# An attention block with a gated feed-forward network: row sums transposed with the mixed tile, a decoding step merged, and a new order

## The chip, the core and the metric

The kernel runs on one core of one Trainium2 chip. The metric is the device time of one execution in microseconds (us). A kernel's time is the median of its runs; the profile is one more execution, with its own time.

The core has engines that each take their instructions in order from a queue of their own and wait for each other by semaphores: TensorE (PE in the profile; PEld is its loading of weights), VectorE (DVE), ScalarE (ACT), GpSimd (POOL) and SyncE (SP), which here issues most of the DMAs.

## What is computed

For 8 batches of 8 heads, 576 positions and head size 64, the reference rotates q and k, takes the softmax of their scaled products, multiplies by v, and sends the result through a feed-forward network with a causal gate of five taps:

```python
    q_rot, k_rot = (rotate(q), rotate(k))
    scale = 1.0 / np.sqrt(D)
    scores = scale * np.matmul(q_rot, k_rot.transpose(0, 1, 3, 2))
    scores = scores - np.max(scores, axis=-1, keepdims=True)
    attn = np.exp(scores)
    attn = attn / (np.sum(attn, axis=-1, keepdims=True) + 1e-09)
    return np.matmul(attn, v).astype(np.float32)
...
    x = np.ascontiguousarray(attn_out.transpose(0, 2, 1, 3)).reshape(B, S, H * D)
...
    for k in range(K):
        gate_pre += conv_w[k][None, None, :] * xp[:, k:k + S, :]
    gate = 1.0 / (1.0 + np.exp(-gate_pre))
    val = x @ w_val
    return (gate * val @ w_out).astype(np.float32)
```

The weights w_val, conv_w and w_out come as float64. The kernel reads their bits as pairs of 32-bit integers and builds float32 from them on the chip: this is "the decoding".

## The kernel before

**Pairs and batches.** Two heads make a pair; there are 32 pairs, four to a batch. A pair's 576 queries of each head are cut into nine tiles of 128 rows: four for each head, and one *mixed* tile (`pm`) that holds the last 64 queries of both heads. For each tile PE computes the scores (`s_mm`, L304: products of high and low parts, half the rows of PE for each head, 128 x 288), DVE takes the negative row maximum (`s_max`, L310), ACT takes the exponential into a tile `p` and adds each row up into a column of `sums` (`s_exp`, L323).

**Transposes.** P has to be transposed for the product with v. PE does it against the identity (`ident`, L338) into a bank of PSUM named `ps_t`; ACT (L379) or DVE (L381) copies the bank to the tiles `pt0` and `pt1`. The keys of a tile go in four pieces of 128 (`t0` to `t7`, `tm`); the remaining 64 keys of each head in the transposes `th0`, `th1` (keys of four tiles) and `thm` (`hm`, for the mixed tile: one transpose of its last 128 keys, of which the lower 64 rows are used).

**Row sums.** When all nine columns of a pair's sums are there, DVE adds 1e-9 and takes the reciprocal (`r_inv`, L404 and L405), PE transposes the 128 x 128 tile `sums` into a bank of its own (`r_mm`, L409, `ps_r`), ACT copies 16 rows (`r_copy`, L415), SP writes nine rows to DRAM and reads them back, spread over the partitions, into `rb` (`r_write`, `r_read`: one write and three reads). The last pair does this in two groups.

**Product with v and network.** `pv_mm` (L393, `ps_a`) multiplies with v, DVE normalises with `rb` into `x` (L432), ACT and POOL split x into a high and a low part (`xh`, `xl`), ACT and DVE compute the gate (L454, L457, L462). When a batch's four pairs are done, the network's first product runs on PE in 96 matmuls (`f_mm`, L480, `ps_f<-xh,wval_hi` and the like), DVE multiplies with the gate (L488), ACT and POOL split y (L492, L495), and 96 matmuls more give the output (`ps_f<-y,wout_hi`), scaled by ACT (L502) or DVE (L504). All of `ps_t`, `ps_r`, `ps_a` and `ps_f` share four banks in turn.

**Rotation.** q and k arrive by DMA in `qin` and `kin`; POOL, and for a part DVE, multiply and add (L276, L280), ACT and POOL or DVE split the result (L283, L287).

**Decoding.** `decode` (L516 to L530) builds float32 from the bits in seven steps, then splits it into `w_hi` (ACT) and `w_lo`. Steps four and five compare the exponent with the smallest normal one (L520) and multiply by the answer (L521). Steps five, nine and ten run on DVE or POOL, by a flag for each block. w_val comes in four blocks of 512 columns, w_out in eight of 256.

**The order.** No engine's order is written out. Every step is a job with an engine, a duration as the planner sees it, what it reads and writes, and a due time. The planner plays the jobs through and writes down the order in which each engine takes them; the due times and the choices of engine come from the table `DUE` (L30) and, for pairs 0 to 4 and batch 0, from its entries with `@e`. Where the planner sees PE idle in the first part of the run, it writes transposes of the identity into the gap (`fill`, L331), called fillers below. So a change of `DUE` changes the order on every engine, and neither arithmetic nor data.

Of the kernel before, what the change touches and what calls it, by code (L numbers as in the profile page):

```python
# [10 lines left out]
F32 = mybir.dt.float32  # L11
# [4 lines left out]
ALU = mybir.AluOpType  # L16
# [3 lines left out]
S = 576  # L20
D = 64
# [180 lines left out]
def attn_gated_ffn(ctx: ExitStack, tc: tile.TileContext, q2, k2, v2, tab, w_val, conv_w, w_out, out, collect=None):  # L202
# [42 lines left out]
    state = {}  # L245
# [66 lines left out]
    def s_exp(p, i):  # L312
        st = state[p]
        if i < 8:
            c, h = i // 2, i % 2
            if f"p{c}" not in st:
                st[f"p{c}"] = pp.tile([128, 2, S], F32, name="p", tag="p")
            pd = st[f"p{c}"][:, h]
            col = c + 5 * h
        else:  # L320
            pd = st["pm"] = pp.tile([128, 2, S], F32, name="p", tag="p")[:, 0]
            col = 4
        A.activation(out=pd.rearrange("p (b x) -> p b x", b=2), in_=st[f"s{i}"], func=AF.Exp, bias=st[f"nm{i}"], scale=1.0,  # L323
                     accum_out=sums[p % 2][:, col:col + 1])
# [16 lines left out]
    def t_mm(p, key):  # L341


        st = state[p]
        if key == "m":
            transpose(p, key, [(st["pm"][:, j * 128:(j + 1) * 128], 128) for j in range(4)])
        elif key == "hm":
            transpose(p, key, [(st["pm"][:, 448:S], 128)])
        elif key[0] == "h":
            g = int(key[1])  # L350
            transpose(p, key, [(st[f"p{2 * g + n}"].rearrange("p h s -> p (h s)")[:, 512:640], 128) for n in range(2)])
        else:
            c, h = int(key) // 2, int(key) % 2
            transpose(p, key, [(st[f"p{c}"][:, h, h * D + j * 128:h * D + (j + 1) * 128], 128) for j in range(4)])

    def t_copy(p, key, eng):
        st = state[p]
        bank = st["b" + key]
        g = 1 if key in ("m", "hm", "h1", "4", "5", "6", "7") else 0
        n = G1 if g else G0  # L360
        if f"pt{g}" not in st:
            st[f"pt{g}"] = pt.tile([128, 9 * n], F32, name=f"pt{g}", tag=f"pt{g}")
        t = st[f"pt{g}"]
        last = t[:, 8 * n:9 * n]
        if key == "m":
            moves = [(bank.rearrange("p (j h x) -> p j h x", j=4, h=2),
                      t[:, 0:8 * n].rearrange("p (h j x) -> p j h x", h=2, j=4)[:, :, :, 256:320])]
        elif key == "hm":
            moves = [(bank[D:128, HEAD[h]], last[HEAD[h], 256:320]) for h in range(2)]
        elif key[0] == "h":  # L370
            moves = [(bank[:, 0:256], last[:, 0:256])]
        else:
            c, h = int(key) // 2, int(key) % 2
            off = (c - 2 * g) * 128
            moves = [(bank.rearrange("p (j x) -> p j x", j=4),
                      t[:, 0:8 * n].rearrange("p (s x) -> p s x", x=n)[:, h * 4:h * 4 + 4, off:off + 128])]
        for src, dst in moves:
            if eng is A:
                A.copy(out=dst, in_=src)  # L379
            else:  # L380
                V.tensor_copy(out=dst, in_=src)  # L381
# [19 lines left out]
    def r_inv(p, g):  # L401
        for a, b in COLS[g]:
            r = sums[p % 2][:, a:b]
            V.tensor_scalar(out=r, in0=r, scalar1=1e-9, scalar2=None, op0=ALU.add)  # L404
            V.reciprocal(out=r, in_=r)  # L405
# [6 lines left out]
    def r_copy(p, g):  # L412
        st = state[p]
        st[f"rr{g}"] = small.tile([16, 128], F32, name="rr", tag="rr", bufs=B["rr"])
        A.copy(out=st[f"rr{g}"], in_=st[f"br{g}"][0:16, 0:128])  # L415
# [94 lines left out]
    def decode(st, fa, eng, hi_out=None, lo_out=None, whole=None):  # L510

        view = st.rearrange("p (n t) -> p n t", t=2)
        hi, lo = view[:, :, 1], view[:, :, 0]
        fh, wa = hi.bitcast(F32), fa.bitcast(I32)
        steps = [
            lambda: V.tensor_scalar(out=wa, in0=hi, scalar1=0x07FFFFFF, scalar2=3, op0=ALU.bitwise_and,  # L516
                                    op1=ALU.logical_shift_left),
            lambda: V.scalar_tensor_tensor(out=wa, in0=hi, scalar=-0x40000000, in1=wa, op0=ALU.bitwise_and, op1=ALU.bitwise_or),
            lambda: V.tensor_scalar(out=hi, in0=hi, scalar1=0x7FF00000, scalar2=None, op0=ALU.bitwise_and),
            lambda: V.tensor_scalar(out=fh, in0=hi, scalar1=float(0x38100000), scalar2=None, op0=ALU.is_ge),  # L520
            lambda: eng.tensor_tensor(out=fa, in0=fa, in1=fh, op=ALU.mult),  # L521
            lambda: V.tensor_scalar(out=hi, in0=wa, scalar1=-0x00800000, scalar2=None, op0=ALU.bitwise_and),
            lambda: V.scalar_tensor_tensor(out=fh, in0=lo.bitcast(U32), scalar=2.0 ** -52, in1=fh, op0=ALU.mult, op1=ALU.mult),  # L523
        ]
        if whole is not None:
            return steps + [lambda: V.tensor_tensor(out=whole, in0=fa, in1=fh, op=ALU.add)]
        return steps + [
            lambda: A.copy(out=hi_out, in_=fa),
            lambda: eng.tensor_tensor(out=fa, in0=fa, in1=hi_out.bitcast(F32), op=ALU.subtract),
            lambda: eng.tensor_tensor(out=lo_out, in0=fa, in1=fh, op=ALU.add),  # L530
        ]
# [67 lines left out]
    for i in range(8):  # L599
        at("dtap", 5.3 + 0.4 * i, "G" if i == 4 else "V", 190 if i == 4 else 90, lambda i=i: taps[i](), w="cw oo/taps0 oo/taps1",  # L600
           port=i in (1, 6, 7))

    def weights(n):
        for i in range(4 if n == "val" else 8):
            x = 512 if n == "val" else 256
            tok = f"y{1 - i % 2}/w{i}" if n == "val" else f"wst/{i}"
            at(f"l{n}{i}", 0, "SP", 650, load_weight, n, i, w=tok, kb=x * 1.024)
            v, v2, g = x * 0.522 + 67, x * 1.045 + 67, x * 2.18 + 105
            eg = ("V", v2) if O.get(f"e{n}{i}") else ("G", g)
            for k, (e, ns) in enumerate((("V", v), ("V", v2), ("V", v), ("V", v), eg, ("V", v), ("V", v2),  # L610
                                         ("A", x * 0.83 + 94), eg, eg)):
                at(f"d{n}{i}", k * 0.5, e, ns, weight_step, n, i, k, w=tok + f" w{n}{i}" * (k in (7, 9)), port=e == "V")

    for p in range(NP):
# [32 lines left out]
        for c in range(5):  # L647
# [154 lines left out]
```

## Time and profile before

| | us |
|---|---|
| median of 3 runs | 789.59 (788.5 to 789.95) |
| the profiled execution | 784.94 |
| its span, first to last instruction | 783.2 |
| busy in it: PE / DVE / ACT / POOL | 750.3 / 606.9 / 488.6 / 415.9 |

A profile's row of a group gives line, engine, operation, what is written and read, shape and count, then the busy time of the group, the mean duration in ns, and the engine's idle time just ahead of it with what ended it. A row of the timeline begins with start and duration in us. A row of waits gives engine and tile, what was waited for, and then the total in us, the number of waits and the longest. PE's matmuls overlap: the next one starts while the one before still runs, so its cost is the step from start to start and not its duration.

### The profile page before, as it was taken

To read this page: it belongs to the slowest core of one execution; us is meant where nothing else is said; L and a number is where in the kernel's file an instruction comes from. 1 tells how busy PE (TensorE), PEld (TensorE's weight loads), DVE (VectorE), ACT (ScalarE), POOL (GpSimd) and SP (SyncE) were. 2 spreads that over 40 slices of the span, in tenths; PEclk is the share of its full clock that TensorE was granted. 3 is DMA by queue.
4 is the path that set the end of the run, shared out by engine and by line. 5 is a ranking of instruction groups with operands and counts; after the bars stand their busy time and mean duration, and the time that the engine had idled before them with its cause. 6 is when DMAs were issued, how large, how long until landed. Compare 5 with 4: busy or idle time off the path is not lost.

```text
span 783.2 us, 16858 instructions
## 1 busy us (share of the span) xinstructions
PE 750.3 (96%) x6284; PEld 616.0 (79%) x6284; DVE 606.9 (77%) x994; ACT 488.6 (62%) x1155; POOL 415.9 (53%) x300
## 2 busy tenths in 40 slices
PE   8889789899999999999999999999999999999998
PEld 8766666578778887887778787887878788878798
DVE  5898989999877887778687887778687876876640
ACT  2565647556566676766666766766666766766532
POOL 2556535455666664567555664467556664551121
PEclk9999989999999999999999999999999999999999
DMA  7654313432343333432443343323343334410111
GB/s 189 158 123 128 82 45 94 127 82 73 90 116 94 94 101 95 108 84 64 116 116 101 89 112 102 102 72 71 109 116 107 91 106 110 114 30 24 33 42 62
DMA packets 92884, 73.81 MB, mean 94 GB/s; under 512 B 60633, under 2 KB 71426, under 8 KB 92802
## 3 DMA queue, kind: packets, MB, share of 16 engines
q1 hardware_dynamic: 91250, 71.51, 34.4%
q10 hardware_dynamic: 1552, 1.21, 0.7%
q8 instruction: 50, 0.82, 0.4%
q14 instruction: 32, 0.26, 0.1%
HBM read 63.10 MB, written 9.59 MB: 93 GB/s over the span
## 4 chain that ended last, share of the span: by engine, by line
PE 67%; DVE 21%; DMA 4%; ACT 4%; issue 3%; SPq 1%; POOL 1%; POOLq 0%; ACTq 0%; DVEq 0%
PE ps_f L480 21%; PE ps_a L393 15%; PE ps_s L304 14%; PE ps_t L338 14%; DVE nm L310 5%; DVE g L457 5%; ACT p L323 2%; DMA kin<-in_k 2%; DVE sums L404 2%; DVE pt L381 1%; PE ps_t L331 1%; DMA qin<-in_q 1%; DVE y L488 1%; DVE k L287 1%; DVE wst L523 1%
## 5 line engine op out<-in xcount | busy, mean ns | idle before, releaser
L323 ACT ACTIVATE p<-ps_s,nm 128x576 f32<-128x576 f32 x288 | 211.9, 739 | 117.2 <-DVE nm L310 114.7
L310 DVE TENSOR_REDUCE nm<-ps_s 128x1 f32<-128x576 f32 x288 | 208.9, 750 | 53.7 <-PE ps_s L304 52.3
L338 PE MATMUL ps_t<-ident,p 128*128 128x128 f32 x1312 | 191.4, 279 | 15.7 <-ACT p L323 9.5
L338 PEld LDWEIGHTS ps_t<-ident,p 128*128 128x128 f32 x1312 | 146.2, 141 | 50.5 <-issue 20.4
L304 PE MATMUL ps_s<-k,q 64*128 64x288 f32 (+1 forms) x1728 | 172.5, 309 | 4.3 <-ACT p L323 3.1
L393 PE MATMUL ps_a<-pt,v 128*64 128x320 f32 (+1 forms) x1280 | 170.5, 411 | 0.0
L304 PEld LDWEIGHTS ps_s<-k,q 64*128 64x128 f32 (+1 forms) x1728 | 135.2, 185 | 33.7 <-issue 18.9
L276 POOL TENSOR_TENSOR qin<-qin,tab_q 128x640 f32<-128x640 f32 x62 | 102.3, 1660 | 95.6 <-DMA qin<-in_q 95.6
L379 ACT COPY pt<-ps_t 128x512 f32<-128x512 f32 (+2 forms) x261 | 118.8, 466 | 27.5 <-PE ps_t L338 24.8
L393 PEld LDWEIGHTS ps_a<-pt,v 128*64 128x64 f32 x1280 | 85.8, 136 | 60.9 <-issue 10.1
L457 DVE SCALAR_TENSOR_TENSOR g<-x,cw,g 128x576 f32<-128x576 f32 (+2 forms) x132 | 118.2, 899 | 1.7 <-ACT g L454 1.4
L480 PE MATMUL ps_f<-y,wout_hi 128*128 128x288 f32 (+2 forms) x512 | 111.1, 304 | 2.4 <-ACT pt L379 2.4
L381 DVE COPY pt<-ps_t 128x512 f32<-128x512 f32 (+1 forms) x155 | 97.0, 629 | 10.3 <-PE ps_t L338 10.2
L287 POOL TENSOR_TENSOR q<-qin,q 128x640 fp32r<-128x640 f32 (+1 forms) x32 | 52.7, 1648 | 69.3 <-ACT q L283 63.9
L480 PEld LDWEIGHTS ps_f<-y,wout_hi 128*128 128x128 f32 x512 | 82.5, 189 | 5.0 <-ACT pt L379 3.5
L444 POOL TENSOR_TENSOR xl<-x,xh 128x576 fp32r<-128x576 f32 (+2 forms) x33 | 45.6, 1383 | 73.1 <-ACT xh L440 59.9
L495 POOL TENSOR_TENSOR y<-y,y 128x288 fp32r<-128x288 f32 (+2 forms) x64 | 54.2, 848 | 54.2 <-ACT y L492 54.1
L480 PE MATMUL ps_f<-xh,wval_hi 128*128 128x288 f32 (+2 forms) x256 | 77.9, 304 | 0.4 <-DVE x L432 0.3
L480 PE MATMUL ps_f<-xl,wval_hi 128*128 128x288 f32 (+2 forms) x256 | 77.2, 302 | 0.0
L480 PE MATMUL ps_f<-y,wout_lo 128*128 128x288 f32 (+2 forms) x256 | 77.1, 301 | 0.0
L480 PE MATMUL ps_f<-xh,wval_lo 128*128 128x288 f32 (+2 forms) x256 | 76.0, 297 | 0.0
L280 POOL TENSOR_TENSOR kin<-kin 128x640 f32<-128x640 f32 (+1 forms) x32 | 49.9, 1558 | 34.9 <-DVE kin L276 34.0
(74 smaller groups left out, 886.1 us busy)
## 6 DMA issues: line engine op xcount, KB each, us to landing
kin<-in_k SPq DMA_DIRECT2D x62, 288.0 KB, 3.9
qin<-in_q SPq DMA_DIRECT2D x31, 512.0 KB, 4.1
out_t<-o SPq DMA_DIRECT2D x56, 144.0 KB, 2.6
rb<-rd SPq DMA_DIRECT2D x31, 144.0 KB, 3.6
v<-in_v SPq DMA_DIRECT2D x32, 128.0 KB, 2.2
v<-in_v SPq DMA_DIRECT2D x64, 64.0 KB, 2.3
rb<-rd SPq DMA_DIRECT2D x31, 128.0 KB, 3.1
qin<-in_q SPq DMA_DIRECT2D x64, 32.0 KB, 3.0
```

Of the source, the lines that this page charges most:

```text
L276: eng.tensor_tensor(out=t[:, i, a:b], in0=t[:, i, a:b], in1=tabs[n][:, i, a:b], op=ALU.mult)
L287: eng.tensor_tensor(out=t[:, 1], in0=ins[n][:, 0, a:b], in1=t[:, 0].bitcast(F32), op=ALU.subtract)
L304: T.matmul(out=tiles[h][:, half, 0:288], lhsT=st["q"][rows, x, c * 128:c * 128 + 128], rhs=st["k"][rows, y, k0:k0 + 288], start=(i == 0), ...
L310: V.tensor_reduce(out=st[f"nm{i}"], in_=st[f"s{i}"], axis=AX.XY, op=ALU.max, negate=True)
L323: A.activation(out=pd.rearrange("p (b x) -> p b x", b=2), in_=st[f"s{i}"], func=AF.Exp, bias=st[f"nm{i}"], scale=1.0, accum_out=sums[p % 2 ...
L338: T.transpose(out=bank[0:rows, j * 128:(j + 1) * 128], in_=src, identity=ident)
L379: A.copy(out=dst, in_=src)
L381: V.tensor_copy(out=dst, in_=src)
L393: T.matmul(out=acc[HEAD[h], 0:n], lhsT=st["v"][:, j, h, :], rhs=st[f"pt{g}"][:, at_:at_ + n], start=(j == 0), stop=(j == 4))
L457: V.scalar_tensor_tensor(out=g, in0=x_sb[:, a + k:b + k], scalar=w, in1=g, op0=ALU.mult, op1=ALU.add)
L480: T.matmul(out=acc[:, 0:n], lhsT=wt[w][:, kc, ds], rhs=mv, start=(kc == 0 and i == 0), stop=(kc == NCH - 1 and i == 2))
L495: G.tensor_tensor(out=ffn[b][1][:, dc, lo:hi], in0=ffn[b, "y", dc, lo], in1=ffn[b][0][:, dc, lo:hi].bitcast(F32), op=ALU.subtract)
```

## The change

**Row sums.** For every pair but the last the reciprocal now goes to nine columns behind the mixed tile's keys (the tile's second half is free), and the transpose `hm` takes the mixed tile's last 64 keys and these nine columns together: 73 columns, one bank. Its rows 0 to 63 go to `pt1` as before, its rows 64 to 72 are the transposed sums that ACT copies for the write. The separate transpose stays only in the last pair. The transpose `hm` now also waits for the reciprocal, and the reciprocal stands in the list of jobs ahead of the transposes.

**Decoding.** Comparison and product are one `scalar_tensor_tensor` on DVE (12 blocks of weights, and the taps).

**Plan.** Of the 431 numbers in `DUE`, 317 are others, and 75 are new. Among them are choices of engine: from pair 5 on the copy of `t1` goes from DVE to ACT (27 copies), of the output scalings DVE has 39 in place of 22 and ACT the fewer, one block of w_val and one of w_out go from POOL to DVE in the decoding and another of w_out the other way, and in pair 0 some halves of the rotation change between DVE and POOL. There are 398 fillers in place of 395.

```diff
-            transpose(p, key, [(st["pm"][:, 448:S], 128)])
+            n = D if p == NP - 1 else D + 9
+            transpose(p, key, [(st["pmt"].rearrange("p h s -> p (h s)")[:, 512:512 + n], n)])
...
-            moves = [(bank[D:128, HEAD[h]], last[HEAD[h], 256:320]) for h in range(2)]
+            moves = [(bank[0:D, HEAD[h]], last[HEAD[h], 256:320]) for h in range(2)]
...
-            V.reciprocal(out=r, in_=r)
+            V.reciprocal(out=r if p == NP - 1 else state[p]["pmt"][:, 1, a:b], in_=r)
...
-        A.copy(out=st[f"rr{g}"], in_=st[f"br{g}"][0:16, 0:128])
+        if p == NP - 1:
+            A.copy(out=st[f"rr{g}"], in_=st[f"br{g}"][0:16, 0:128])
+        else:
+            A.copy(out=st[f"rr{g}"][0:9], in_=st["bhm"][D:D + 9, 0:128])
...
-            lambda: V.tensor_scalar(out=fh, in0=hi, scalar1=float(0x38100000), scalar2=None, op0=ALU.is_ge),
-            lambda: eng.tensor_tensor(out=fa, in0=fa, in1=fh, op=ALU.mult),
+            lambda: V.scalar_tensor_tensor(out=fa, in0=hi, scalar=float(0x38100000), in1=fa, op0=ALU.is_ge, op1=ALU.mult),
...
+        last = p == NP - 1
+        if not last:
+            at("rinv", t, "V", 450, r_inv, p, None, r=toks(f"sums{par}#@", range(9)) + f" p/{p}.m", w=f"p/{p}.m#r sums{par}#r")
...
-                r = f"p/{p}.m"
+                r = f"p/{p}.m" + f" p/{p}.m#r" * (key == "hm" and p < NP - 1)
```

Three places of the order show what moves. On PE, in the middle of the run, at the end of a pair's transposes (`ps_r` is the transpose of the sums, the single `ps_t` behind it is `hm`, `ps_f` is the network), before:

```order
L304 MATMUL ps_s<-k_86,q_88 128x288 x12
L338 MATMUL ps_t<-ident,p 128x128 x4
L409 MATMUL ps_r<-ident,sums_102 128x128
L338 MATMUL ps_t<-ident,p 128x128
L480 MATMUL ps_f<-xh,wval_hi 128x288
L480 MATMUL ps_f<-xl,wval_hi 128x288
```

and now, at a like place (`73x128` is `hm` with the sums):

```order
L304 MATMUL ps_s<-k_86,q_88 128x288 x12
L339 MATMUL ps_t<-ident,p 128x128 x4
L339 MATMUL ps_t<-ident,p 73x128
L485 MATMUL ps_f<-y_5410,wout_hi 128x288
L485 MATMUL ps_f<-y_5411,wout_hi 128x288
```

The transpose of the sums is gone, and the one behind it stands where it stood.

On PE in the opening, the network's first matmul, before: it stands behind scores of the seventh pair (360 score matmuls ahead of it) and the product with v of the sixth (`ps_a`).

```order
L409 MATMUL ps_r<-ident,sums_102 128x128
L338 MATMUL ps_t<-ident,p 128x128 x4
L393 MATMUL ps_a<-pt_1833,v_92 64x256 x4
L304 MATMUL ps_s<-k_86,q_88 128x288 x12
L393 MATMUL ps_a<-pt_1833,v_92 64x256 x6
L338 MATMUL ps_t<-ident,p 128x128 x4
L393 MATMUL ps_a<-pt_1938,v_92 64x320 x10
L304 MATMUL ps_s<-k_86,q_88 128x288 x12
L480 MATMUL ps_f<-xh,wval_hi 128x288
```

Now it stands behind the fifth pair's last scores (270 score matmuls ahead of it); the row without `p` is a filler:

```order
L304 MATMUL ps_s<-k_86,q_88 128x288 x12
L332 MATMUL ps_t<-ident 128x128 x15
L339 MATMUL ps_t<-ident,p 128x128 x4
L304 MATMUL ps_s<-k_86,q_88 128x288 x6
L339 MATMUL ps_t<-ident,p 128x128 x6
L485 MATMUL ps_f<-xh,wval_hi 128x288
```

The network begins 90 score matmuls earlier in PE's queue.

On DVE, the last piece of w_val's low part (`wval_lo`), which the network's first matmul needs; `nm` is a row maximum, `g` a tap of the gate, `wst` a block under decoding. Before it is the 259th instruction, behind 58 maxima:

```order
L523 SCALAR_TENSOR_TENSOR wst<-wst 128x512
L310 TENSOR_REDUCE nm<-ps_s 128x1
L529 TENSOR_TENSOR wst<-wst,wval_hi 128x512
L310 TENSOR_REDUCE nm<-ps_s 128x1
L381 COPY pt_2122<-ps_t 128x4x128
L516 TENSOR_SCALAR wst<-wst 128x256
L530 TENSOR_TENSOR wval_lo<-wst 128x512
```

Now it is the 210th, behind 44 maxima:

```order
L527 SCALAR_TENSOR_TENSOR wst<-wst 128x512
L526 TENSOR_SCALAR wst<-wst 128x256
L276 TENSOR_TENSOR kin<-kin,tab_k 128x640
L527 SCALAR_TENSOR_TENSOR wst<-wst 128x256
L533 TENSOR_TENSOR wst<-wst,wval_hi 128x512
L462 SCALAR_TENSOR_TENSOR g<-x_100,cw,g 128x576
L534 TENSOR_TENSOR wval_lo<-wst 128x512
```

The decoding of w_val moved 49 instructions forward on DVE. Of the row maxima, the 54th moved from place 234 to 253, and the 63rd from 289 to 287.

More of the change, by code (lines that the diff above doesn't have):

```diff
@@ L320, in s_exp @@
         else:
-            pd = st["pm"] = pp.tile([128, 2, S], F32, name="p", tag="p")[:, 0]
+            st["pmt"] = pp.tile([128, 2, S], F32, name="p", tag="p")
+            pd = st["pm"] = st["pmt"][:, 0]
             col = 4
@@ L598, in attn_gated_ffn @@
     at("taps", -49, "SP", 650, load_taps, w="cw oo/taps0 oo/taps1", kb=20)
-    for i in range(8):
-        at("dtap", 5.3 + 0.4 * i, "G" if i == 4 else "V", 190 if i == 4 else 90, lambda i=i: taps[i](), w="cw oo/taps0 oo/taps1",
-           port=i in (1, 6, 7))
+    for i in range(7):
+        at("dtap", 5.3 + 0.4 * i, "V", 90, lambda i=i: taps[i](), w="cw oo/taps0 oo/taps1", port=True)
     def weights(n):
@@ L609, in weights @@
             eg = ("V", v2) if O.get(f"e{n}{i}") else ("G", g)
-            for k, (e, ns) in enumerate((("V", v), ("V", v2), ("V", v), ("V", v), eg, ("V", v), ("V", v2),
+            for k, (e, ns) in enumerate((("V", v), ("V", v2), ("V", v), ("V", v2), ("V", v), ("V", v2),
                                          ("A", x * 0.83 + 94), eg, eg)):
-                at(f"d{n}{i}", k * 0.5, e, ns, weight_step, n, i, k, w=tok + f" w{n}{i}" * (k in (7, 9)), port=e == "V")
+                at(f"d{n}{i}", k * 0.5, e, ns, weight_step, n, i, k, w=tok + f" w{n}{i}" * (k in (6, 8)), port=e == "V")
     for p in range(NP):
@@ L669, in attn_gated_ffn @@
             at(f"c{key}", t + w, e, ns, t_copy, p, key, V if va else A, r=b, w=f"pt{g}/{p}#{key}")
-        last = p == NP - 1
         cols = {None: range(9), 0: (0, 1, 2, 3), 1: range(4, 9)}
@@ L673, in attn_gated_ffn @@
             k = "l" + str(g) if last else ""
-            at("rinv" + k, t, "V", 250 * (1 + last), r_inv, p, g, r=toks(f"sums{par}#@", cols[g]), w=f"sums{par}#r")
-            at("rmm" + k, t, "PE", 110, r_mm, p, g, r=f"sums{par}#r", w=f"ps_t/r{p}{g}", mode="f")
-            at("rcp" + k, t, "A", 260, r_copy, p, g, r=f"ps_t/r{p}{g}", w=f"rr/{p}{g}")
+            if last:
+                at("rinv" + k, t, "V", 500, r_inv, p, g, r=toks(f"sums{par}#@", cols[g]), w=f"sums{par}#r")
+                at("rmm" + k, t, "PE", 110, r_mm, p, g, r=f"sums{par}#r", w=f"ps_t/r{p}{g}", mode="f")
+            at("rcp" + k, t, "A", 260, r_copy, p, g, r=f"ps_t/r{p}{g}" if last else f"ps_t/{p}hm", w=f"rr/{p}{g}")
             at("rw" + k, t, "SP", 650, r_write, p, g, r=f"rr/{p}{g}", w=f"rd/{p}{g}", kb=100)
```

2 lines of the change are left out of this document (1 added, 1 removed).

## The prediction

> **What bounds the kernel now.** I read the page first, then busy time by stretch, then what the matmul engine waits for, then single places of the timeline. The page gives span and engines:
>
> ```profile
> span 783.2 us, 16858 instructions
> PE 750.3 (96%) x6284; PEld 616.0 (79%) x6284; DVE 606.9 (77%) x994; ACT 488.6 (62%) x1155; POOL 415.9 (53%) x300
> ```
>
> 96% for PE hides two different stages, so I cut the span. Columns: stretch, length, then busy us and instructions of PE, PEld, DVE, ACT, POOL, then the granted clock, DMA share and GB/s.
>
> ```profile
> 0.00:20.00 20.00, 17.23 (x136) 16.33 (x136) 11.20 (x35) 4.58 (x9) 5.76 (x12) 1.00 0.76 188
> 20.00:40.00 20.00, 17.23 (x155) 15.06 (x154) 16.29 (x28) 11.25 (x28) 10.49 (x8) 1.00 0.64 161
> 40.00:80.00 40.00, 34.90 (x298) 25.83 (x296) 35.69 (x60) 23.87 (x54) 23.74 (x17) 1.00 0.47 121
> 80.00:120.00 40.00, 33.31 (x267) 27.54 (x269) 37.20 (x55) 21.95 (x52) 18.73 (x12) 0.91 0.24 61
> 120.00:200.00 80.00, 71.84 (x600) 55.62 (x598) 75.98 (x127) 48.57 (x115) 44.27 (x31) 1.00 0.35 96
> 200.00:300.00 100.00, 98.49 (x832) 80.60 (x828) 77.97 (x124) 65.50 (x156) 62.30 (x45) 1.00 0.38 98
> ```
>
> From 200 us on PE is full and DVE has a fifth of its time free: here the time is the number of matmuls times their step. Before 200 us DVE is 93 to 95% full (40 to 200 us), and much of PE's busy time is the filler (395 transposes of the identity). What PE itself waits for says the same; in the opening (0 to 205 us) eleven rows, from the first to the last of these, add up to 25.8 us:
>
> ```profile
> PE ps_t L338 <- ACT p L323: 9.4, 9, 1.8
> PE ps_t L338 <- DVE x L432: 5.3, 2, 3.6
> ...
> PE ps_s L304 <- DVE k L287: 0.2, 1, 0.2
> ```
>
> and from 205 to 760 us the first row below is 2.4 of 3.4 us in all:
>
> ```profile
> PE ps_f L480 <- ACT pt L379: 2.4, 5, 0.5
> PE ps_r L409 <- DVE sums L405: 0.4, 1, 0.4
> ```
>
> So a matmul less after 200 us is worth its whole step, an operation less on ACT or POOL nothing, and the opening hangs on how DVE's queue feeds PE.
>
> **The removed transposes.** The order has 33 transposes of the sums before and 2 after (the last pair's). One costs its step to the next start, not its duration:
>
> ```profile
> 414.14 0.66 PE L338 MATMUL ps_t<-ident,p 128*128 128x128 f32 x4
> 414.63 0.27 PE L409 MATMUL ps_r<-ident,sums 128*128 128x128 f32 x1
> 414.74 0.27 PE L338 MATMUL ps_t<-ident,p 128*128 128x128 f32 x1
> ...
> 418.31 0.29 PE L480 MATMUL ps_f<-xh,wval_lo 128*128 128x288 f32 x1
> 418.44 0.30 PE L480 MATMUL ps_f<-xh,wval_hi 128*128 128x288 f32 x1
> 418.67 0.53 PE L304 MATMUL ps_s<-k,q 64*128 64x288 f32 x4
> ```
>
> 414.63 to 414.74 is 0.11 us. 25 of the 31 stand behind the opening (closed below at the seventh pair's last scores): 25 x 0.11 = **-2.75 us**. The transpose that now carries the sums stood right behind the removed one, so it waits for nothing that wasn't waited for there already; with 73 columns in place of 128 its step is bounded by 0 and these 0.11 us, and I take it as unchanged. The new wait (this transpose on the reciprocal) has the same PE queue behind it as the old one. The 9 x 128 copy to SBUF, the write and the two reads of the sums stay: as many DMAs, of the same sizes, on SP.
>
> Every removed transpose also gave up one of the four banks of ps_t. Right behind one PE waits for a bank:
>
> ```profile
> 284.72 0.27 PE L338 MATMUL ps_t<-ident,p 128*128 128x128 f32 x1
> 285.46 0.54 PE L480 MATMUL ps_f<-y,wout_hi 128*128 128x288 f32 x2 [0.47 <-ACT pt L379]
> ```
>
> This is the row of five waits, 2.4 us, above. With a bank less in turn it may go entirely (-2.4) or come back elsewhere (0); I take half, **-1.2 us**. Matmuls of half the rows (ps_s) start 0.23 us after the one before (418.44 to 418.67) where others step 0.13 (418.31 to 418.44): a change of form costs 0.10 us. Behind the 96th FFN matmul the order has three such changes fewer: **-0.3 us**.
>
> **The decoding.** The group rows (busy us, mean ns):
>
> ```profile
> L520 DVE TENSOR_SCALAR wst<-wst 128x256 f32<-128x256 int32 x8 | 3.8, 470 | 0.0
> L520 DVE TENSOR_SCALAR wst<-wst 128x512 f32<-128x512 int32 x4 | 1.7, 428 | 0.0
> L521 DVE TENSOR_TENSOR wst<-wst 128x256 f32<-128x256 f32 x6 | 3.8, 637 | 0.0
> L521 DVE TENSOR_TENSOR wst<-wst 128x512 f32<-128x512 f32 x3 | 2.1, 684 | 0.0
> L518 DVE SCALAR_TENSOR_TENSOR wst<-wst 128x256 int32<-128x256 int32 x8 | 4.7, 585 | 0.0
> L518 DVE SCALAR_TENSOR_TENSOR wst<-wst 128x512 int32<-128x512 int32 x4 | 4.1, 1017 | 0.0
> L529 DVE TENSOR_TENSOR wst<-wst,wval_hi 128x512 f32<-128x512 f32 x3 | 4.2, 1415 | 0.0
> L530 DVE TENSOR_TENSOR wval_lo<-wst 128x512 fp32r<-128x512 f32 x3 | 3.4, 1138 | 0.0
> ```
>
> DVE loses 3.8 + 1.7 + 3.8 + 2.1 = 11.4 us. The merged step isn't in the trace; L518 has its shape and operand places: 8 x 0.585 + 4 x 1.017 = 8.7 us. Bounds: L521's 637 and 684 (7.8 us) and L518's 1017 for all (12.2). The order also moves two steps of one block of w_val from POOL to DVE (4.2/3 + 3.4/3 = 2.5 us). Net -0.2 us on DVE, between -1.1 and +3.3: the shorter decoding frees POOL, not DVE.
>
> **The plan.** DVE's average instruction in the first 200 us is 176.4/305 = 0.58 us (the windows' sums). The last piece of w_val is DVE's 259th instruction before and its 210th after, that is near 120 + 32/127 x 80 = 140 us; the 54th row maximum moves from 234 to 253 (+11 us), the 63rd from 289 to 287. So the first FFN matmul can come 30 us earlier,
>
> ```profile
> 173.76 0.41 PE L480 MATMUL ps_f<-xh,wval_hi 128*128 128x288 f32 x1
> ```
>
> and the pairs' scores later in between. I close the opening at the last scores of the seventh pair (63rd maximum). Up to there both orders hold the same number of score and value matmuls and of transposes of p (378, 120 and 272). The new order has 12 FFN matmuls more (1.6 us at 0.13), 10 fillers more (1.1) and 6 transposes of the sums less (0.7): PE's queue is 2.0 us longer there and leaves 1.6 us less behind. With the 25.8 us of waits as they are: **+0.4 us**. From both sides: waits halved, -12.5; scores 11 us late with nothing to cover it, +11.
>
> 27 copies to pt go from DVE to ACT and 17 output scalings the other way:
>
> ```profile
> L381 DVE COPY pt<-ps_t 128x512 f32<-128x512 f32 x123 | 83.8, 683 | 4.2 <-PE ps_t L338 4.0
> L379 ACT COPY pt<-ps_t 128x512 f32<-128x512 f32 x165 | 94.9, 586 | 22.6 <-PE ps_t L338 22.3
> L504 DVE TENSOR_SCALAR o<-ps_f 128x288 f32<-128x288 f32 x22 | 10.0, 454 | 12.3 <-PE ps_f L480 12.3
> L502 ACT ACTIVATE o<-ps_f 128x288 f32<-128x288 f32 x34 | 14.1, 413 | 13.5 <-PE ps_f L480 9.3 <-issue 3.9 <-ACT pt L379 0.2
> ```
>
> ACT gains 27 x 0.575 - 17 x 0.415 = 8.5 us over 585 us, DVE loses 10.7. PE, full at 98.5 of 100 us, hides both; without that cover the 8.5 us would be the cost.
>
> **Sum.** -2.75 - 1.2 - 0.3 + 0.4 = -3.9 us. The profiled execution took 784.94 us, so 781.0 for one like it. The three runs' median is 789.59, 4.65 above the profiled one; I keep that distance: 785.7.
>
> **Rivals.** (1) *The opening's waits shrink.* For it: the largest is one accident. DVE's decoding steps
>
> ```profile
> 103.59 1.76 DVE L521 TENSOR_TENSOR wst<-wst 128x256 f32<-128x256 f32 x1
> 105.27 2.02 DVE L518 SCALAR_TENSOR_TENSOR wst<-wst 128x512 int32<-128x512 int32 x1
> ```
>
> ran at two to three times their usual length beside POOL,
>
> ```profile
> 105.14 1.60 POOL L280 TENSOR_TENSOR qin<-qin 128x640 f32<-128x640 f32 x1
> ```
>
> and PE stood still until DVE came to the normalisation behind them:
>
> ```profile
> 109.49 1.11 PE L338 MATMUL ps_t<-ident,p 128*128 128x128 f32 x4 [3.62 <-DVE x L432]
> ```
>
> Against it: the new decoding starts earlier, beside the same rotation work of POOL. Waits reduced by 8 us give -12, 777.6 us. The Trainium skill, GPSIMD Engine Reference, Specifications, says that POOL shares its SBUF interfaces with VectorE and contends with its instructions that have two SBUF inputs; these rows agree, and the merged step is such an instruction. By that rule it would take about 1.9 us instead of 0.6 wherever POOL runs; if that were all twelve, 12 x 1.3 = 16 us more of DVE in the opening, which would make rival 3 the outcome.
>
> (2) *Nothing is left of it.* For it: ACT's extra copies hold banks longer, and its queue is where the bank was waited for. If the old bank wait stays (1.2 us against my sum) and one more of 0.47 us comes in each of the six later batches of four pairs (2.8 us), the 3.9 us are gone: 789.6 us. Against it: ACT is free for a third of that time (65.50 of 100 us busy).
>
> (3) *Slower: decoding ahead of the maxima starves PE.* PE takes its queue in order; behind a transpose that waits for scores the FFN matmuls wait too. The maxima up to the 54th come up to 11 us later in DVE's queue, and the order covers it with fillers alone (369 of them stand ahead of the first FFN matmul; it was 388 in an order that reached it 30 us later). It decides where the opening's waits pass 25.8 + 3.9 = 30 us; at 34 us the kernel takes 793.6. The accident above had a tail, too:
>
> ```profile
> 106.00:110.00 4.00, 0.51 (x3) 0.52 (x4) 4.00 (x8) 0.28 (x1) 0.74 (x1) 0.73 0.29 66
> 110.00:115.00 5.00, 5.00 (x26) 4.99 (x25) 3.68 (x9) 2.35 (x5) 0.00 (x0) 0.53 0.19 52
> ```
>
> The clock fell to 0.53 after it, so 5 us of PE's time did half the work; another such gap while PE has real work costs 2.5 us on top. The Trainium skill, TensorE: Matmul & The Clock Gate, "What's actually happening", gives an idle window of about 3.4 us as the limit for half rate; the gap of 3.62 us agrees.
>
> **How the numbers follow.** Forecast (-1.6 to -8.5 us, 781 to 788): 0.48. Rival 1: 0.15. Rival 2: 0.18. Rival 3: 0.19. A change under 0.2% (1.6 us) can't be told from none in this kernel. Faster 0.48 + 0.15 = 0.63, same 0.18, slower 0.19. The range runs from rival 1's price to rival 3's, 777.5 to 793.5, and leaves out less than half of each, some 0.15.
>
> **What would show it.** No ps_r before the last pair, and PE at 98 to 99% from 200 us on with steps of 0.11 and 0.13 us: the removed transposes. No wait of ps_f for ACT's pt in every batch: the bank. First FFN matmul between 140 and 150 us, PE's waits to 205 us near 26 us: the opening; over 30 us, rival 3; under 18, rival 1. The merged step at 0.4 to 1.0 us: the decoding. The forecast is wrong if PE waits after 205 us for ACT's exp or pt by more than 6 us in all.

## The result, and the profile after

| | before | after |
|---|---|---|
| median of 4 runs each, us | 789.05 (787.69 to 789.95) | 768.14 (767.01 to 770.02) |
| ratio, with its 95% interval | | 0.9739 (0.9714 to 0.9764) |
| the profiled execution, us | 784.94 | 768.52 |
| its span, us | 783.2 | 766.7 |

The kernel is 20.9 us faster; 3.9 were forecast, and the time lies below the range. Two executions of kernels further down, of 830.08 and 925.51 us, ran at a granted clock of 0.847 and 0.752; they count in their medians but in no ratio, and the profile taken of the first isn't read. The page of the changed kernel, span and engines:

```profile
span 766.7 us, 16713 instructions
PE 742.0 (97%) x6256; PEld 614.0 (80%) x6256; DVE 576.6 (75%) x978; ACT 495.8 (65%) x1165; POOL 402.4 (52%) x293
```

Busy time by stretch, columns as before:

```profile
0.00:20.00 20.00, 17.40 (x131) 16.54 (x131) 9.66 (x32) 3.32 (x6) 4.84 (x10) 1.00 0.77 196
40.00:80.00 40.00, 37.75 (x323) 28.43 (x324) 36.41 (x64) 26.68 (x63) 22.85 (x15) 1.00 0.40 106
80.00:120.00 40.00, 34.05 (x292) 26.15 (x290) 36.40 (x55) 23.62 (x56) 18.16 (x11) 1.00 0.32 80
120.00:200.00 80.00, 73.39 (x603) 58.96 (x601) 72.46 (x121) 50.29 (x118) 45.80 (x33) 0.98 0.38 93
200.00:300.00 100.00, 100.00 (x860) 84.06 (x857) 75.38 (x123) 72.05 (x170) 59.36 (x42) 1.00 0.38 101
```

In the last stretch PE starts 860 matmuls where it started 832. What PE waits for from 205 us on:

```profile
PE ps_r L411 <- DVE sums L407: 0.2, 1, 0.2
PE ps_t L339 <- ACT pt L381: 0.2, 1, 0.2
```

That is all: 0.4 us of 3.4 are left, and the row "ps_f <- ACT pt" is gone. The largest waits up to 205 us (seven rows, 20.5 us in all, against 25.8):

```profile
PE ps_t L339 <- ACT p L324: 6.1, 9, 1.8
PE ps_t L339 <- DVE p L407: 4.0, 3, 2.0
PE ps_s L304 <- ACT p L324: 4.0, 5, 1.3
PE ps_f L485 <- DVE wval_lo L534: 3.7, 1, 3.7
```

The second row is the wait that the change adds (the mixed tile's transpose on the reciprocal); before, "ps_r <- DVE sums" stood there with 2.8 us up to the seventh pair's last scores. The fourth comes from starting the network early. The timeline of PE, the first matmul of the network and the one that waits, and the 288th:

```profile
134.57 0.38 PE L485 MATMUL ps_f<-xh,wval_hi 128*128 128x288 f32 x1
...
139.61 0.40 PE L485 MATMUL ps_f<-xh,wval_lo 128*128 128x288 f32 x1 [3.73 <-DVE wval_lo L534]
...
275.02 0.29 PE L485 MATMUL ps_f<-xh,wval_lo 128*128 128x288 f32 x1
```

**Where the time went.** Two places on PE cut every profile alike: the seventh pair's last scores (378 score matmuls, the prediction's end of the opening) and the network's 288th matmul, from which on PE has no gap to fill. The last column works out the opening that belongs to a kernel's median: the median, less 1.8 us that lie around the span (784.94 - 783.2 and 768.52 - 766.7), less the stage from the 288th matmul on.

| profile of | 378th score, us | 288th network matmul | end | from one to the other | 288th to end | median, us | opening by the median |
|---|---|---|---|---|---|---|---|
| before | 189.7 | 282.9 | 783.2 | 93.2 | 500.3 | 789.1 | 287.0 |
| before, again | 194.3 | 287.5 | 786.6 | 93.2 | 499.1 | 789.3 | 288.4 |
| after | 187.1 | 275.0 | 766.7 | 87.9 | 491.7 | 768.1 | 274.6 |
| after, again | 190.6 | 279.3 | 771.2 | 88.7 | 491.9 | 768.6 | 274.9 |

The columns of differences repeat within about 1 us; the opening up to the 378th score moves by 4 us from one execution to the next. The first profile of before was among its shortest executions (784.94, where 46 others of it, timed beside the experiments, gave 784.74 to 793.61), the second profile of after was the longest of its six (772.98). The two profiles near their medians, before again and after, differ by 19.9 us: 7.2 up to the 378th score, 5.3 from there to the 288th matmul, 7.4 behind it.

The opening can be cut once more. Neither order has a network matmul ahead of the 270th score. Between that score and the 378th the old order holds 76 of them, all behind the 360th score, and the new one 88, most of them ahead of it. The waits are PE's, in us; the last column is the time in which the granted clock was 0.50.

| profile of | 270th score, us | from there to the 378th | network matmuls and fillers in between | waits up to the 378th | at half clock up to there |
|---|---|---|---|---|---|
| before | 137.6 | 52.2 | 76 and 36 | 24.8 | 6.8 |
| before, again | 140.4 | 53.9 | 76 and 36 | 26.3 | 10.2 |
| after | 133.9 | 53.3 | 88 and 29 | 20.5 | 3.4 |
| after, again | 136.1 | 54.5 | 88 and 29 | 21.0 | 10.2 |

So the stretch into which the network moved got no shorter that can be seen. What the new order gains up to the 378th score it gains ahead of the 270th.

**The clock in the opening.** It falls to 0.50 for some 3.4 us at a time, or twice that. The stretches of before and of after, columns as above:

```profile
107.80:114.60 6.80, 5.11 (x23) 5.10 (x24) 5.48 (x13) 1.95 (x4) 0.00 (x0) 0.50 0.16 44
```

```profile
140.10:143.50 3.40, 3.40 (x17) 3.40 (x16) 3.32 (x7) 1.00 (x2) 0.00 (x0) 0.50 0.21 62
```

Each lies at a long wait of PE: the first around the one of 3.62 us that the prediction quotes, the second right behind the one of 3.73 us. How many there are differs from one execution to the next, and the time goes with it. For 58 executions of before the mean granted clock is on record: the 13 with 0.987 took 790.15 to 793.61 us, the six with 0.996 took 785.55 to 788.34, and a straight line through all gives 6.1 us for 0.01. How far the clock is the cause and how far the long waits are isn't shown. Before has 0.991 on average and after 0.995, so by that line some 2 of the 20.9 us go with the clock (an estimate).

### The profile page after: what moved, and what is told of

The parts are those of the page before. It is cut to its first block, busy times and chain, and to the rows that moved or that the text cites. A ratio compares the mean times of both kernels' runs of the same rounds, so it can differ in the third digit from the quotient of the medians.

```text
span 766.7 us, 16713 instructions
## 1 busy us (share of the span) xinstructions
PE 742.0 (97%) x6256; PEld 614.0 (80%) x6256; DVE 576.6 (75%) x978; ACT 495.8 (65%) x1165; POOL 402.4 (52%) x293
## 4 chain that ended last, share of the span: by engine, by line
PE 83%; DVE 9%; DMA 4%; SPq 1%; ACT 1%; issue 1%; DVEq 0%; ACTq 0%
PE ps_f L485 27%; PE ps_a L395 19%; PE ps_t L339 18%; PE ps_s L304 18%; DMA kin<-in_k 3%; DVE nm L310 2%; DVE g L462 2%; PE ps_t L332 1%; DMA wst<-in_w_val 1%; DVE k L287 1%; DVE wst L533 1%; DVE kin L276 1%; SPq L259 1%; ACT p L324 1%; DVE sums L406 1%
## 5 line engine op out<-in xcount | busy, mean ns | idle before, releaser
L339 PE MATMUL ps_t<-ident,p 128*128 128x128 f32 (+1 forms) x1312 | 182.3, 277 | 11.2 <-ACT p L324 6.1
L381 ACT COPY pt<-ps_t 128x512 f32<-128x512 f32 (+2 forms) x288 | 131.0, 479 | 68.4 <-PE ps_t L339 67.3
L339 PEld LDWEIGHTS ps_t<-ident,p 128*128 128x128 f32 (+1 forms) x1312 | 145.1, 141 | 37.3 <-issue 15.1
L395 PE MATMUL ps_a<-pt,v 128*64 128x320 f32 (+1 forms) x1280 | 168.0, 410 | 0.0
L304 PEld LDWEIGHTS ps_s<-k,q 64*128 64x128 f32 (+1 forms) x1728 | 134.3, 185 | 37.9 <-issue 24.7
L462 DVE SCALAR_TENSOR_TENSOR g<-x,cw,g 128x576 f32<-128x576 f32 (+2 forms) x132 | 120.2, 911 | 2.7 <-ACT g L459 1.9
L276 POOL TENSOR_TENSOR qin<-qin,tab_q 128x640 f32<-128x640 f32 x62 | 98.6, 1612 | 11.7 <-DMA qin<-in_q 11.7
L287 POOL TENSOR_TENSOR q<-qin,q 128x640 fp32r<-128x640 f32 (+2 forms) x33 | 54.3, 1645 | 76.8 <-ACT q L283 76.8
L280 POOL TENSOR_TENSOR kin<-kin 128x640 f32<-128x640 f32 (+1 forms) x32 | 51.7, 1616 | 65.4 <-DVE kin L276 63.7
L383 DVE COPY pt<-ps_t 128x512 f32<-128x512 f32 (+1 forms) x128 | 77.2, 615 | 3.9 <-PE ps_t L339 3.8
```

What stands on the lines that cost most here:

```text
L276: eng.tensor_tensor(out=t[:, i, a:b], in0=t[:, i, a:b], in1=tabs[n][:, i, a:b], op=ALU.mult)
L287: eng.tensor_tensor(out=t[:, 1], in0=ins[n][:, 0, a:b], in1=t[:, 0].bitcast(F32), op=ALU.subtract)
L304: T.matmul(out=tiles[h][:, half, 0:288], lhsT=st["q"][rows, x, c * 128:c * 128 + 128], rhs=st["k"][rows, y, k0:k0 + 288], start=(i == 0), ...
L339: T.transpose(out=bank[0:rows, j * 128:(j + 1) * 128], in_=src, identity=ident)
L395: T.matmul(out=acc[HEAD[h], 0:n], lhsT=st["v"][:, j, h, :], rhs=st[f"pt{g}"][:, at_:at_ + n], start=(j == 0), stop=(j == 4))
L462: V.scalar_tensor_tensor(out=g, in0=x_sb[:, a + k:b + k], scalar=w, in1=g, op0=ALU.mult, op1=ALU.add)
```

## The experiments

Each ratio is to the kernel before, timed in the same series on the same chip (its medians there: 789.76, 791.22 and 789.47 us). A ratio of 0.001 is 0.8 us. An interval reaches 2 to 3 us either way, so a difference of two of these ratios is uncertain by some 3 us; the stage behind the 288th matmul, which repeats within about 1 us, says more. Three of the expectations (with 496.7, 496 and 488.2 us) count that stage to the start of PE's last matmul, 3.6 us before the end of the span.

| kernel | median, us (runs) | ratio | 95% interval | 288th to end, us |
|---|---|---|---|---|
| before, again | 789.33 (12) | 1.0004 | 0.9979 to 1.0029 | 499.1 |
| after, again | 768.62 (6) | 0.9741 | 0.9709 to 0.9773 | 491.9 |
| after, own transpose and bank | 771.89 (6) | 0.9784 | 0.9756 to 0.9812 | 494.6 |
| after, own transpose, shared bank | 772.23 (6) | 0.9779 | 0.9751 to 0.9807 | |
| after, decoding in two steps | 773.17 (6) | 0.9793 | 0.9764 to 0.9822 | 492.0 |
| before, shared bank | 788.28 (12) | 0.9979 | 0.9954 to 1.0004 | 499.0 |
| before, without the addition | 783.90 (7) | 0.9915 | 0.9886 to 0.9944 | 495.5 |
| after, without the addition | 765.93 (6) | 0.9688 | 0.9659 to 0.9716 | 491.9 |
| before, both edits | 783.11 (6) | 0.9917 | 0.9887 to 0.9948 | 497.2 |
| after, batch 0's network late | 783.87 (6) | 0.9922 | 0.9891 to 0.9953 | 491.7 |
| after's jobs, before's numbers | 885.49 (6) | 1.1205 | 1.1169 to 1.1241 | 619.4 |

**The two kernels again**, unchanged, for the spread and a second profile of each:

> The kernel before once more, with a second profile. Between its profiled execution (784.94 us) and the median of its runs (789.05) lie 4.1 us, while the changed kernel's profiled execution (768.52) lies 0.4 us from its median. Theory A (an execution of before varies in the opening, by waits of PE and drops of the clock there): the profile shows span and opening different from the first one, and from 283 us (the 288th network matmul) to the end the same 496.7 us within 0.5. Theory B (variation lies in the stage where PE is full): the difference shows after 283 us.

> The changed kernel once more, on the chip and beside the runs of before that the other two have: 768 us, its stage behind the 288th network matmul 491.7 us within 0.5, and its opening (to that matmul) 275 us within 2.

They are in the tables above: from one execution to the next the opening varies by over 4 us, the stage behind it by about 1, which is more than the 0.5 expected.

**The separate transposes put back into the new order**, once in a bank of their own and once into the mixed tile's bank. The order on all engines stays; PE has 31 instructions more.

```diff
-            n = D if p == NP - 1 else D + 9
+            n = D
+            if p < NP - 1:
+                r_mm(p, None)
```

> The changed kernel in its own order, but with a separate transpose of the sums in a bank of its own right ahead of hm, as before. Theory A (the gain after the opening is the 31 transposes plus the bank that each held): 31 x 0.11 = 3.4 us, and the waits for a bank come back, in each batch some 0.7 to 1.2 us, in all 8 to 11 us over the changed kernel, 776 to 779 us. Rival (the waits of before came from its order, not from the bank): 3.4 us over, 771.5 us.

For the second kernel the transpose goes to the second quarter of the bank that `hm` uses:

```diff
+            if p < NP - 1:
+                T.transpose(out=st["bhm"][:, 128:256], in_=sums[p % 2], identity=ident)
```

> As a1_own_bank, but the separate transpose of the sums goes to the second quarter of hm's bank, so no bank more is held. Both theories: 31 x 0.11 = 3.4 us over the changed kernel (771.5 us), without new waits for a bank; the difference to a1_own_bank is what the bank is worth (A: 5 to 8 us, rival: 0).

Against the changed kernel's 0.974 they cost 0.0044 and 0.0039, or 3.5 and 3.1 us (their intervals and the changed kernel's overlap a little); 31 transposes of 0.11 us are 3.4. In the first one the stage from the 288th matmul on, which holds 21 of them, is 2.8 us longer than in the changed kernel (494.6 against 491.8, the mean of two). The bank makes no difference that can be seen: the rival was right, and theory A's 8 to 11 us did not come. PE's waits in the kernel with own banks, from 205 to 760 us:

```profile
PE ps_t L339 <- ACT p L324: 0.3, 2, 0.2
PE ps_r L413 <- DVE sums L409: 0.2, 1, 0.2
PE ps_t L339 <- DVE x L436: 0.2, 1, 0.2
PE ps_t L339 <- ACT pt L383: 0.2, 1, 0.2
```

These are all. The old wait of ps_f for the bank does not come back, though the bank is used again. So the bank was not its cause.

**One bank less in the old order**, the other half of that question: the sums are transposed into `hm`'s bank, everything else as before.

```diff
-        bank = psT.tile([128, 512], F32, name="ps_r", tag="ps_t")
-        T.transpose(out=bank[:, 0:128], in_=sums[p % 2], identity=ident)
+        if "bhm" not in st:
+            st["bhm"] = psT.tile([128, 512], F32, name="ps_t", tag="ps_t")
+        to = st["bhm"][:, 128:256]
+        T.transpose(out=to, in_=sums[p % 2], identity=ident)
```

> The kernel before in its own order, with the transposes of the sums in the second quarter of hm's bank, so that one bank less is taken for each pair and nothing else changes. Theory B (my prediction's: the bank is what PE waits for): the 0.7 us at the start of each batch's second network product goes, 4 us less, 785 us. Theory P (the copies behind the stalled step are late whatever the bank): within 1.5 us of 789.5.

The wait at the bank does vanish. PE's timeline at the place that the prediction quotes with 0.47 us of idle time:

```profile
287.74 0.27 PE L338 MATMUL ps_t<-ident,p 128*128 128x128 f32 x1
...
287.77 0.51 PE L487 MATMUL ps_f<-y,wout_hi 128*128 128x288 f32 x2
```

The step is 0.03 us where it was 0.74 (284.72 to 285.46). Yet the kernel takes 788.28 us, as theory P had it, and the stage 499.0 us as before, because PE's weight loads now wait one station later, ahead of the scores. Their waits from 205 to 760 us, here and then in the kernel before:

```profile
PEld ps_s L304 <- ACT p L323: 4.5, 11, 0.8
```

```profile
PEld ps_s L304 <- ACT p L323: 1.8, 6, 0.5
```

Something upstream is late, and the bank is only where PE meets it.

**What is late.** The old timeline around that wait, all engines in order of time:

```profile
281.66 2.19 POOL L287 TENSOR_TENSOR q<-qin,q 128x640 fp32r<-128x640 f32 x1
...
282.66 1.23 DVE L404 TENSOR_SCALAR sums<-sums 128x9 f32<-128x9 f32 x1 [0.23 <-ACT p L323]
...
284.05 0.41 DVE L488 SCALAR_TENSOR_TENSOR y<-g,ps_f 128x288 f32<-128x288 f32 x1
...
284.49 0.43 ACT L492 CAST y<-y 128x288 fp32r<-128x288 f32 x1 [0.82 <-DVE y L488]
...
284.83 0.58 ACT L379 COPY pt<-ps_t 128x512 f32<-128x512 f32 x1
```

Read it upwards from PE's 285.46. The copy that frees the bank starts at 284.83, behind the cast of y on ACT, which waited 0.82 us for y from DVE. DVE was late with y because an addition of 1e-9 to nine columns (L404) took 1.23 us. It ended at 283.89, POOL's instruction at 283.85. Of the 31 such additions 27 start while POOL runs an instruction; each ends 0.03 to 0.04 us behind that one, whether it took 0.17 or 1.53 us. The four others take 0.16 or 0.17. In the new order 15 of 31 start beside POOL, and from 205 us on none takes more than 0.45 us. The group rows, before and after (busy us, mean ns):

```profile
L404 DVE TENSOR_SCALAR sums<-sums 128x9 f32<-128x9 f32 x31 | 19.7, 635 | 5.3 <-ACT p L323 5.3
```

```profile
L406 DVE TENSOR_SCALAR sums<-sums 128x9 f32<-128x9 f32 x31 | 11.9, 383 | 1.5 <-ACT p L324 1.4
297.26 0.16 DVE L406 TENSOR_SCALAR sums<-sums 128x9 f32<-128x9 f32 x1
```

(The last line is one of the timeline, an addition with POOL idle.) The Trainium skill, SBUF — State Buffer, "Who interferes with whom", says that an operation of this kind which uses both of DVE's ports and an instruction of GpSimd exclude each other for the whole instruction. These rows agree, even at nine columns.

**Without the addition, in both orders.** A row's sum is at least 1, since its largest exponential is 1, so 1e-9 is lost in float32; the kernels leave that addition out.

```diff
-            V.tensor_scalar(out=r, in0=r, scalar1=1e-9, scalar2=None, op0=ALU.add)
```

> The kernel before in its own order, without the step that adds 1e-9 to the row sums (L404; a row's sum is at least 1, where 1e-9 is lost in float32). In the trace of before each L404 that starts while POOL computes ends about 0.03 us after POOL's instruction does, up to 1.5 us long. Theory P (this stall delays y's product on DVE, y's copy on ACT and the copy of pt behind it, and so is the 0.7 us that PE loses at the start of each batch's second network product): from the 288th network matmul to the end 496 us become 491 to 492, and the opening 1 to 3 us shorter: 781 to 785 us in all, against 789.5. Rival (the waits come from the bank or from the order elsewhere): the rest within 1 us of 496, in all 787 to 789.

> The changed kernel in its own order without the step that adds 1e-9 (L406). Theory P (after the opening its order keeps these stalls off PE's path): the rest, 488.2 us from the 288th network matmul on, within 0.5 us, and the opening 0 to 3 us shorter: 765.5 to 768.5 us. Rival (PE still loses by them): 762 to 765.

In the old order this brings 0.0085, 6.7 us, of which 4.2 lie behind the 288th matmul (499.7, the mean of two, to 495.5). PE's waits there from 205 to 760 us:

```profile
PE ps_r L408 <- DVE sums L404: 0.2, 1, 0.2
PE ps_s L304 <- ACT p L323: 0.2, 1, 0.2
```

With bank, transposes and order as before, the wait "ps_f <- ACT pt" is gone: the stall made it. The addition's own 0.16 us isn't the reason, since in the new order, where it is seldom held, the same edit changes nothing behind the 288th matmul (491.9). There it brings 0.0052, 4 us, in all, and so in the opening. This last kernel, at 765.93 us, is the fastest of the study; it wasn't timed in one series with the changed kernel, and the intervals of the two just touch.

**The decoding's two steps put back into the new order:**

```diff
-            lambda: V.scalar_tensor_tensor(out=fa, in0=hi, scalar=float(0x38100000), in1=fa, op0=ALU.is_ge, op1=ALU.mult),
+            lambda: (V.tensor_scalar(out=fh, in0=hi, scalar1=float(0x38100000), scalar2=None, op0=ALU.is_ge),
+                     eng.tensor_tensor(out=fa, in0=fa, in1=fh, op=ALU.mult)),
```

> The changed kernel in its own order, but the merged decoding step is two again (comparison on DVE, product on DVE or POOL by the block's flag). Theory A (the shorter decoding gave the opening its gain): DVE gets 12 steps back, 8 x 0.25 + 4 x 0.42 = 3.7 us by their shortest durations, more beside POOL, and the run is 3 to 6 us longer (771 to 774). Rival (the opening's gain is the new order alone): within 1.5 us of the changed kernel.

It costs 0.0053, 4.2 us, all of it in the opening (492.0 behind it), as theory A expected. Its six executions had a mean clock of 0.992 where the changed kernel's had 0.995; by the line above that goes with 1 to 2 of the 4.2 us. The merged step itself, in the changed kernel:

```profile
L525 DVE SCALAR_TENSOR_TENSOR wst<-wst 128x256 f32<-128x256 int32 x8 | 3.3, 414 | 0.0
L525 DVE SCALAR_TENSOR_TENSOR wst<-wst 128x512 f32<-128x512 int32 x4 | 2.8, 711 | 0.0
```

That is 6.1 us in place of the 11.4 that L520 and L521 took on DVE.

**Both edits in the old order**, the sums with `hm` for pairs 6 to 29 and the merged step, with the table of before:

> The kernel before in its own order with both edits made there: the merged decoding step (its second half emits nothing), and for pairs 6 to 29 the sums in hm and no transpose of their own (in the other pairs hm stands ahead of the reciprocal in that order). Theory E (edits and order each bring their part): 24 x 0.11 = 2.6 us and the 5.0 us of the decoding step, 781 to 783 us against 790 for before, and the stalls of L404 stay: the stage behind the 288th network matmul takes 499.7 - 2.5 = 497 us. Rival (the edits are all, the new order only lets them in): 768 to 774 us. Second rival (in the old order the decoding's end isn't what PE waits for): 787 us.

It brings 0.0083, 6.6 us, a third of the change: 2.5 us behind the 288th matmul (499.7 to 497.2), where 20 of its 24 removed transposes stand (20 x 0.11 = 2.2), and the rest in the opening. The other two thirds come with the new order, the choices of engine in it and the seven transposes that stay here.

**Batch 0's first network product held back.** The new order on every engine but for this product and what directly follows it (the gating and splitting of y), which wait until the seventh pair's third group of scores; the fillers are written by the times planned before these jobs were moved.

```diff
+        early = lambda i: self.jobs[i][3].__name__ in ("f_mm", "y_mul", "y_hi", "y_lo") and self.jobs[i][4][0] == 0 and (
+            self.jobs[i][3].__name__ != "f_mm" or self.jobs[i][4][1] == 0)
+        cut = next(k for k, i in enumerate(order) if self.jobs[i][3].__name__ == "s_mm" and self.jobs[i][4] == LATE) + 1
+        order = [i for i in order[:cut] if not early(i)] + [i for i in order[:cut] if early(i)] + order[cut:]
```

> The changed kernel, but batch 0's first network product is held back until the third score group of pair 6, where before began it; fillers take the places that become free. Theory E (the early network matmuls use PE time of the opening that is lost otherwise): the 64 to 72 matmuls held back, 8 to 9.6 us at 0.133, have to be done in the full stage: 774 to 778 us. Rival (the opening's gain is DVE's, by the shorter decoding and fewer stalls beside POOL): within 2 us of the changed kernel.

It costs 0.018, 14 us, more than either expectation gave. Its 378th score comes at 200.9 us in place of 187.1, its 288th network matmul at 288.6, and behind that it is the changed kernel (491.7). PE's groups up to the 378th score, in the changed kernel and then here (fillers and the network's `xh,wval_hi`):

```profile
L332 PE MATMUL ps_t<-ident 128*128 128x128 f32 x398 | 50.8, 284 | 1.4 <-POOL ident masks.py:199 1.4
L485 PE MATMUL ps_f<-xh,wval_hi 128*128 128x288 f32 x30 | 10.0, 335 | 0.0
```

```profile
L337 PE MATMUL ps_t<-ident 128*128 128x128 f32 x561 | 68.0, 277 | 1.4 <-POOL ident masks.py:199 1.4
L490 PE MATMUL ps_f<-xh,wval_hi 128*128 128x288 f32 x30 | 9.0, 301 | 0.0
```

The work that counts is the same, 88 network matmuls included (30 + 29 + 29), and so are the waits (19.1 us against 20.5). The difference is 163 fillers, 17.9 us at 0.11. By stretches:

| kernel | 270th to 360th score, us | network matmuls and fillers in it | 360th to 378th | network matmuls and fillers in it |
|---|---|---|---|---|
| before | 36.0 | 0 and 36 | 16.2 | 76 and 0 |
| after | 46.2 | 76 and 17 | 7.1 | 12 and 12 |
| after, network late | 44.2 | 0 and 113 | 24.7 | 88 and 79 |

In the first stretch 96 fillers (10.6 us) took the place of 76 network matmuls (10.1 us), so it could hardly get shorter; before needs 36.0 us for the same scores with 36 fillers. In the second, 67 fillers stand in one row between two network matmuls of one group:

```profile
186.51 0.29 PE L490 MATMUL ps_f<-xh,wval_hi 128*128 128x288 f32 x1
186.90 7.53 PE L337 MATMUL ps_t<-ident 128*128 128x128 f32 x67
194.19 0.38 PE L490 MATMUL ps_f<-xl,wval_hi 128*128 128x288 f32 x1
```

The matmul behind them reads tiles that were in use before and goes on in a bank already begun; nothing but the row holds it, for 7.3 us. The fillers come from planned times that no longer hold. So this kernel shows what misplaced fillers cost, and not that the early network stands where PE's time is lost otherwise; without its added fillers it was not run. That before, with the network at the late place, needs 52.2 and 53.9 us from the 270th to the 378th score, and after 53.3 and 54.5, speaks against a gain from the place. Its granted clock is the highest of all:

```profile
core 0: 780.3 us, clock 0.999
```

A full clock alone, then, doesn't make the opening short.

**The new jobs with the old table of numbers**, everything else as after:

> The changed jobs (sums in hm, merged decoding step) with the due times of before, so planned again but not tuned. Theory N (the new due times carry most of the gain): 780 to 786 us, the 3.8 and 5.0 us of the two edits at most. Rival (the edits carry it, and any plan would do): 768 to 774 us.

94 us slower than before (885.49 against 791.22); both expectations were far off. PE's two largest waits over the whole span:

```profile
PE ps_t L339 <- ACT p L324: 56.6, 48, 2.2
PE ps_s L304 <- ACT p L324: 21.3, 18, 3.0
```

The table's due times belong to one list of jobs; taken over for another list, they put 48 transposes and 18 scores on PE ahead of the exponentials that these wait for. No part of the change can be priced from this kernel.

## Why the prediction was wrong

The direction was right; the forecast of 785.7 us and its range were not. Step by step:

- **What bounds the kernel**: right. PE is full from 200 us on (100.00 of 100), and DVE's time is on the opening's path (the decoding below).
- **Removed transposes, -2.75 us**: right. Put back, all 31 cost 3.1 to 3.5 us; 2.8 behind the 288th matmul, where 21 x 0.11 = 2.3 were to be expected. (The reads of the sums that stay are three, not two.)
- **The bank, -1.2 us, bounds 0 and -2.4**: wrong in cause and in size. The step that failed was "Every removed transpose also gave up one of the four banks of ps_t. Right behind one PE waits for a bank". The bank itself is worth nothing that can be seen in either order; the lateness came from the addition of 1e-9 that stood behind POOL, and it cost 4.2 us. The row of L404 with 635 ns for nine columns was in the profile, and the prediction never priced it. The size was also bounded by the wrong view: the wait's row counts idle time from modelled ends (0.47 us), while the step from start to start is 0.74 in place of 0.11, so 0.63 us were lost, and a loss ahead of scores shows in the weight loads' rows rather than in PE's.
- **Changes of form, -0.3**: not tested by itself. 7.9 us went behind the 288th matmul; 2.8 (transposes) and 4.2 (the stall) leave 0.9 for it and all else.
- **Opening, +0.4 us**: this term is the larger miss. The step that failed was "With the 25.8 us of waits as they are". PE's queue up to the 378th score was counted right, 2.0 us longer (only the matmuls with v are 240 in either order, not 120). But from before, again, to after PE's waits up to there went from 26.3 to 20.5 us, and the time at half clock from 10.2 to 3.4 us, which is 3.4 us of clock: 2.0 - 5.8 - 3.4 = -7.2 us, as measured. The three other pairs of profiles come out within 1.4 us by the same sum. The waits became fewer ahead of the 270th score, where the 5.3 us for x are gone. From the 378th score to the 288th matmul "leaves 1.6 us less behind" was too little for the 5.3 us measured: 12 network matmuls, 7 fillers and 4 transposes of the sums fewer explain 12 x 0.133 + 11 x 0.11 = 2.8, the waits that are gone there (0.6 + 0.4 + 0.4) another 1.4; 1.1 us stay open.
- **Decoding, -0.2 us on DVE, hidden**: mis-sized. The merged step was priced by L518 at 585 and 1017 ns and measured 414 and 711; L518's means held stalls beside POOL. DVE lost 5.3 us where 2.7 were allowed (11.4 less 8.7), and undoing it costs 4.2 us of the whole, not 0: in the opening DVE's time is on the path, where the prediction had the shorter decoding free POOL alone.
- **Copies and scalings exchanged between DVE and ACT, 0**: right as far as it shows. ACT's row of PE's waits behind 205 us is 0.2 us.
- **Distance of 4.65 us between profile and median**: keeping it came to taking the sum from the median, and did no harm. It belongs to the first profile of before, one of its shortest executions; the changed kernel's profile lay at its median (768.52 against 768.14).
- **Rivals.** The first, that the opening's waits shrink, is what happened there, though by 4 to 6 us and not 8, and with fewer stretches at half clock, which it didn't price. The second (nothing left) expected the bank's wait to come back, which it didn't. The third feared PE's starving and half clock: that came once, in the 3.73 us for wval_lo and the 3.4 us at half clock behind them, while the waits in all fell. The merged step's mean was 0.41 and 0.71 us, not 1.9; but only three of the twelve met a POOL instruction for more than 0.1 us, so the rule that the prediction weighed was hardly put to the test.

What stays open is which of the new due times and choices of engine shortened the opening's waits. Shown by experiment are the stage behind the 288th matmul (2.8 for the transposes and 4.2 for the stall, of 7.9 us) and, for the opening, the merged step (4.2 us when undone). The rest of the opening's 12 to 14 us is accounted for by sums from traces alone.

## What to carry to other kernels

Cut both traces at the same places of one engine's queue and see which stretch got shorter, before a part of the change is given the credit: here it wasn't the stretch into which the network moved. Count the time at half clock in each profile before two openings are compared, and take a second profile. Where work is moved in a planned order, look where the fillers that were planned around it end up. Before a wait is blamed on the resource it is met at, follow it upstream until an instruction is longer than its own shortest, and look for a tiny instruction with a large mean. Price a loss by steps from start to start.

## What the hardware showed that was not expected

- A DVE instruction of one SBUF input and nine columns is held until POOL's running instruction ends: 0.16 us free, up to 1.53 beside POOL, its end 0.03 to 0.04 us behind POOL's. Leaving it out is worth 6.7 us of 790 in one order and 4 in the other.
- The reciprocal of the same nine columns is not held: all 31 take 0.21 or 0.22 us, seven of them beside a POOL instruction, as at 283.92 beside one that runs from 283.81 on:

```profile
283.81 1.41 POOL L444 TENSOR_TENSOR xl<-x,xh 128x576 fp32r<-128x576 f32 x1
...
283.92 0.22 DVE L405 RECIPROCAL sums<-sums 128x9 f32<-128x9 f32 x1
```

- Behind the opening, executions of one kernel repeat within about 1 us in 500 (500.3 and 499.1; 491.7, 491.9); in the two profiles of each kernel the rest of the difference is made in the first 290 us, where the stretches at half clock lie.
- Fillers alone hold the clock: over the row of 67 from 186.90 to 194.2 us the granted clock is 1.00.
